# One MoE kernel, four edits: an expert's output rows read, added and written back, a load with another home, a routing step on another engine, and preparation work in other places

## The chip, the core and the metric

The kernel runs on one core of a Trainium2 chip. The metric is the device time of one execution in microseconds (us). The kernel before takes 880.76 us, the median of three runs (879.85 to 880.87). One further execution was profiled; all rows below come from it.

Engines are named as in the profile: PE is TensorE's matmul, PEld its weight load, DVE is VectorE, ACT is ScalarE, POOL is GpSimd, and SP is SyncE, which only issues DMAs here. A "q" behind a name is that engine's sequencer. Each engine works through its own instructions strictly in program order, so an instruction that waits holds everything behind it on its engine.

## The reference, cut to what matters

Three stages follow one another. An attention with 32 memory slots for each head turns q, k, v and phi into 2304 token rows of 512. A gated feed-forward layer (512 to 1536 to 512) follows. Last comes a mixture of eight experts with the two best experts chosen for each token:

```python
logits = x @ w_gate
noisy = logits + log1p(exp(x @ w_noise)) * noise
top2 = argpartition(-noisy, 2, axis=1)[:, :2]     # two experts for each token
top2_w = softmax(noisy[top2])
for e in range(8):
    for k in range(2):
        mask = top2[:, k] == e
        h = maximum(x[mask] @ w1[e], 0)            # 512 -> 1024
        out[mask] += top2_w[mask, k] * (h @ w2[e]) # 1024 -> 512
```

Each token's output row is therefore written by exactly two experts, and the second must add to what the first left.

## The kernel before, in words

**Blocks.** Tokens are worked in NB = 8 blocks of 288. For each block `slot1(i, f)` runs the twelve slices f of the feed-forward layer. Work of neighbouring stages is hung between the matmuls by a hand-written order: `put(i, n, fn, ...)` files a call at place n of block i, and `run(i, n)` issues what is due. Block number 7 is `last`; in it place 2f + 1.99 ends slot f, so 23.9 to 23.95 is the very end of the feed-forward layer.

**Routing** of a block is the list `GATE`: `g_evac`, transposes of the rows (`g_rows`, `g_copy`), logits, a polynomial, the two best experts (`g_top`, `g_pick`), `g_exp`, `g_weight`, `g_spread` (the weights spread over the expert columns of the row tile R, lines 586 to 591), `g_rank` (on PE, line 601: a count of the tokens before each one), `g_place` (lines 604 to 618: the place of each token in its expert's list; line 612 is a product of R on POOL, line 615 overwrites the one-hot tiles that `g_spread` reads), then six `g_scatter` (line 623), indirect DMAs on POOL that write token rows into the expert lists `xs` in DRAM. Each scatter waits for the one before to land. Routing of block k runs inside block k + 1 at the places `AT["gate"][k]`; that of block 7 runs between the units below.

**Units.** Experts 0 and 1 (and the second part of expert 0) are worked in 32 units, `("u", 0)` to `("u", 31)`. A unit is `up2` (line 899: twelve or so products of the expert's first matrix with the transposed rows XT, then the relu on ACT and its low part on DVE, lines 902 and 903) and `down2` of the unit before (line 917). `prep2(n)` (lines 781 to 783) splits the weights for a unit two or more units ahead into a high part on ACT and low parts `ro` and `wl` on DVE. `load_x(e, part)` (lines 847, 849) loads an expert's rows, four DMAs and one for the small columns; `trans_x` and `split_x2` (lines 856, 861, 862) turn and split them. The raw rows of the first parts of experts 0 and 1 share one buffer, tag `xl` of pool `l`, so the second load waits for the transposes of the first. After it on SP's queue stand the weight loads `wb`, before it the stores of row blocks (`store_x`, line 628).

**Pairs.** Experts 2 to 7 take four pairs each, `("s", 0)` to `("s", 23)`; pair p works two slices of expert 2 + p // 4. `pair()` multiplies in a Strassen form (`product`, line 1075) and interleaves the down products (`down_s`, line 1089) of the pair before: `first` and `second` are those. In one pair the order on PE is: two products (A11, S2), `first(0)`, two (A12, S3), `first(1)`, two (S1, A22), `second(0)`, one (S4), `second(1)`. Line 1112 is the ACT copy of the first product, which A12 waits for; line 1115 the DVE sum that S3 waits for; line 1136 the last sum, which the relu at line 1137 waits for. The rows of the expert to come are prepared in these pairs: `load_xs` (lines 972, 975), `trans_xs` (line 984), `sums_xs` on POOL (lines 990 to 994), `high_xs` on ACT (line 1004), `low_xs` on DVE (line 1008); its weights by `sums_ws` (lines 1028 to 1033), `high_ws`, `low_ws`, `high_w2`, `low_w2`.

**Output.** `finish` (line 934 on ACT) scales an output tile and puts it on the list `todo`; `add` (line 941) issues an indirect DMA on POOL that adds the tile to the rows of `out`. Each waits for the one before to land. Expert 7 goes another way: `gather` (line 947) reads the five tiles of old rows into the ring PV, `finish` adds on DVE (line 931), and a plain indirect DMA writes back. The five gathers wait for the last add of expert 6, and the first write waits for all five gathers.

**Homes.** PV is one tile of eight 512-wide rows, tag `X0`, made at the first `rows` call, after the feed-forward layer has read the weights (`places(False)`) that stand under the same tag. Only its rows 0 to 2 are used as a ring at first; rows 3 to 7 take expert 2's raw rows from unit 13 on.

Of the kernel before, what the change touches and what calls it, by code (L numbers as in the profile page):

```python
# [22 lines left out]
DM = 512  # L23
NF1 = 12
E = 8
# [14 lines left out]
    "gate": {  # L40
        0: (3.9, 5.9, 7.9, 7, 9, 9.9, 9.9, 11, 11, 13.9, 15, 15.1, 15.2, 17.9, 25, 27) + NORMAL[16:],
        5: NORMAL[:13] + (15, 17, 19, 21, 21.9, 21.95, 21.96, 23.96, 25, 25.9, 27.9, 29.9, 31.9, 33.9, 35.9),
        6: NORMAL[:13] + (15, 17, 19, 21, 21.9, 21.95, 21.96, 21.97, 23.94),
        7: (1.5, 4, 5, 4.05, 5.05, 6, 3, 6.05, 3.1, 3.5, 3.6, 3.7, 4.1, 5.1, 6.1, 7.1, 7.5, 7.6, 8.1, 8.1, 9, 9.1),
    },
    "s1": {
        1: (21, 21.9, 23.2, 23.5, 23.6, 23.9, 25, 25.9, 27, 27.9, 29, 29.9, 31, 31.9, 33),
# [20 lines left out]
def moe_program(ctx, tc, phi, kv, q, wa, wgn, nz, wb, out):  # L68
# [517 lines left out]
    def g_spread(i):  # L586
        oh1, oh2, sel, w = RT[i]
        s, s2 = small("gs", sh), small("gs2", sh)
        G.tensor_tensor(s, oh1, w[:, 2].to_broadcast(sh), op=OP.mult)
        G.tensor_tensor(s2, oh2, w[:, 3].to_broadcast(sh), op=OP.mult)  # L590
        G.tensor_add(R[i][:, :, DM:DM + E], s, s2)

    PR = {}

# [9 lines left out]
    def g_place(i):  # L604
        oh1, oh2, sel, w = RT.pop(i)
        p = PR.pop(i)
        pos = small("gpos", sh)
        V.tensor_tensor(pos, p[:TT, :NT, :], base[:TT, None, :].to_broadcast(sh), op=OP.add)
        V.tensor_add(base, base, p[:, NT, :])
        ov = R[i][:, :, 528:528 + E]  # L610
        V.tensor_tensor(ov, pos, e_cap[:TT, None, :].to_broadcast(sh), op=OP.is_ge)
        G.tensor_mul(ov, ov, R[i][:, :, DM:DM + E])
        pf = small("gpf", [TT, NT, 2])
        for n, oh in enumerate((oh1, oh2)):
            V.tensor_mul(oh, oh, pos)
# [25 lines left out]
    def put(i, n, fn, *a):  # L641
        fill.setdefault((i, n), []).append((fn, a))
# [196 lines left out]
    def load_x(e, part):  # L839
        (c0, c1), = PARTS[part]  # L840
        pool = pools["l" if part == "a" else "r"]
        XT[e, part] = pool.tile([128, 4, 2, c1 - c0], F32, tag="xt", name="xt", bufs=2)
        if part == "a":
            ML[e] = pools["m"].tile([128, NC, 9], F32, tag="ml", name="ml", bufs=3)
        t = pool.tile([128, (c1 - c0) // 32, 4, 32], F32, tag="xl", name="xl")
        for c in range(4):
            Q.dma_start(t[32 * c:32 * c + 32].rearrange("b j k a -> b j (k a)"),
                        xs[e * T + c0:e * T + c1, 128 * c:128 * c + 128].rearrange("(j b) w -> b j w", b=32))
        Q.dma_start(ML[e][:, c0 // 128:c1 // 128, :],
                    xs[e * T + c0:e * T + c1, DM:DM + 9].rearrange("(c p) w -> p c w", p=128))  # L850
        XL[e, part] = t
# [12 lines left out]
    def index(e, part):  # L864
# [5 lines left out]
            IX[e] = pools["m"].tile([128, NC], I32, tag="ix", name="ix", bufs=3)  # L870
        V.tensor_add(IX[e][:, t], idf, u[:, t])

    def rows(e, part):
        if "all" not in PV:
            PV["all"] = wpool.tile([128, 8, DM], F32, tag="X0", name="pv", bufs=1)
            PV["next"], PV["ring"] = 0, 3
# [43 lines left out]
    def height(e, t):  # L920
        return CAPS - 128 * t if e > 1 and t == NC - 1 else 128
# [3 lines left out]
    def finish(e, tiles):  # L925
        ml = ML[e]
        for t in tiles:
            pv, h = PV[e, t][:height(e, t)], height(e, t)
            w = ml[:h, t, e:e + 1]
            if e == E - 1:  # L930
                V.scalar_tensor_tensor(pv, AC2[e, t][:h], w, pv, op0=OP.mult, op1=OP.add)
                add(e, t)
                continue
            A.activation(pv, AC2[e, t][:h], AF.Copy, scale=w)  # L934
            todo.append((e, t))

    def add(*tile):
        if tile or todo:
# [282 lines left out]
    put(("u", 13), 2.2, load_xs, 2)  # L1221
    for k in range(2):
        for f, h, fn, m in (((17, 1, trans_xs, 0), (18, 1, trans_xs, 1), (18, 2.2, sums_xs, 0), (19, 1, None, 0),
                             (22, 1, None, 1), (22, 1.1, None, 2), (22, 2.3, sums_xs, 1), (23, 1.1, None, 3)),
                            ((23, 2.3, trans_xs, 0), (24, 1, trans_xs, 1), (24, 2.3, sums_xs, 0), (25, 1, None, 0),
                             (26, 1, None, 1), (26, 1.1, None, 2), (26, 2.3, sums_xs, 1), (27, 1.1, None, 3)))[k]:
# [19 lines left out]
    def at(p, h, fn, *a):  # L1246
        put(("s", p), h, fn, *a)

    for p in range(pairs):
# [5 lines left out]
            at(p, 3, load_wb, n + 5)  # L1255
        if p + 1 < pairs:
            at(p, 7, high_w2, p + 1)
        if 0 < p < pairs - 1:
            at(p, 0, sums_ws, p + 1, 0)
            at(p, 0, sums_ws, p + 1, 1)  # L1260
            at(p, 2, sums_ws, p + 1, 2)
            for h, g, k in ((1, 2, "A"), (3, 4, "B"), (3, 5, "C"), (4, 6, "D")):
                at(p, h, high_ws, p + 1, k)
                at(p, g, low_ws, p + 1, k)
        if e + 1 < E:
            if q == 0:
# [158 lines left out]
```

## Time and profile before

| What | Value |
|---|---|
| Median of three runs | 880.76 us (879.85 to 880.87) |
| The profiled execution | 884.36 us |
| Its span, first to last instruction | 882.6 us |
| Mean granted clock of TensorE in the span | 0.983 of full |
| PE busy | 829.9 us (94%) |
| DVE, ACT, POOL busy | 633.2 us, 388.7 us, 242.0 us |

The span is 1.76 us shorter than the profiled execution, and that execution is 3.6 us longer than the median. A busy PE counts the time in which matmuls are in flight. What an idle stretch of an engine costs depends on what waits for it, so the rows are read from PE's own waits backwards.

### The profile page before, as it was taken

Reading aid. Unit: us, or ns where it says so; the run is one execution under the profiler, and the core shown is the slowest. Engines: PE = TensorE matmul, PEld = TensorE weight load, DVE = VectorE, ACT = ScalarE, POOL = GpSimd, SP = SyncE. Lnnn points to the kernel's source line nnn. Section 1 sums busy time; section 2 is a strip of 40 time slices with the busy share of each in tenths; the row PEclk is TensorE's granted clock in tenths of the full one; section 3 lists DMA queues with packets and bytes.
Section 4 is the critical chain, followed back from the end, with each engine's and each line's share of the span. In section 5 each row is a group of like instructions: output and inputs, shape, how many; then the busy total and the mean of one; then the engine's idle time right before and its main releaser. Section 6 shows DMA issues by size and latency. Waiting matters only on the chain.

```text
span 882.6 us, 16296 instructions
## 1 busy us (share of the span) xinstructions
PE 829.9 (94%) x6136; PEld 734.9 (83%) x6136; DVE 633.2 (72%) x1522; ACT 388.7 (44%) x797; POOL 242.0 (27%) x347
## 2 busy tenths in 40 slices
PE   5898999999999999999979999799999999999992
PEld 2676888899989999899869889688888888888881
DVE  4786587676867586857754576688889988888750
ACT  4663555343443343333434545355446554544520
POOL 2000012424342342432133142202415233241241
PEclk9999999999999999999999999899999999999997
DMA  9966628874437453477647953526574744653331
GB/s 327 401 253 220 192 101 302 264 250 135 110 79 219 103 145 84 122 213 192 165 134 208 243 162 80 124 82 135 133 165 97 164 122 113 137 132 105 85 80 60
DMA packets 85079, 142.00 MB, mean 161 GB/s; under 512 B 16432, under 2 KB 41232, under 8 KB 84992
## 3 DMA queue, kind: packets, MB, share of 16 engines
q1 hardware_dynamic: 65712, 100.66, 36.9%
q0 software_dynamic: 19280, 40.22, 19.8%
q8 instruction: 50, 0.82, 0.4%
q14 instruction: 37, 0.30, 0.1%
HBM read 104.07 MB, written 36.77 MB: 160 GB/s over the span
## 4 chain that ended last, share of the span: by engine, by line
PE 79%; DMA 8%; DVE 7%; ACT 2%; issue 2%; SPq 1%; POOL 1%; DVEq 0%; POOLq 0%; ACTq 0%
PE acc L1089 19%; PE ph L1075 15%; PE acc L460 13%; PE pg L427 9%; PE pv L427 7%; PE ph L899 4%; PE acc L917 3%; DMA xl<-xs 2%; PE pp L314 2%; PE acc L456 2%; DMA xs<-R,gidx 2%; PE pkv L285 1%; DMA out<-pv,ix 1%; PE pT L482 1%; PE psc L314 1%
## 5 line engine op out<-in xcount | busy, mean ns | idle before, releaser
L1089 PE MATMUL acc<-ws,hs 128*128 128x512 f32 (+1 forms) x690 | 176.1, 396 | 0.0
L1075 PEld LDWEIGHTS ph<-xh,ws 128*128 128x128 f32 x1008 | 152.4, 190 | 15.3 <-ACT y L1112 6.1
L1075 PE MATMUL ph<-xh,ws 128*128 128x308 f32 x1008 | 159.1, 306 | 5.3 <-ACT y L1112 5.2
L1089 PEld LDWEIGHTS acc<-ws,hs 128*128 128x128 f32 (+1 forms) x690 | 123.4, 185 | 24.6
L941 POOL DMA_INDIRECT out<-pv,ix x40 | 67.5, 1688 | 188.6 <-ACT pv L934 84.5
L460 PE MATMUL acc<-a,ro 128*128 128x288 f32 x576 | 116.3, 294 | 0.0
L427 PE MATMUL pg<-x,pt 128*128 128x288 f32 x576 | 103.3, 314 | 6.4 <-ACT pt L395 4.4
L460 PE MATMUL acc<-a,os 128*128 128x288 f32 x432 | 105.8, 294 | 0.8 <-DVE os L409 0.8
L427 PEld LDWEIGHTS pg<-x,pt 128*128 128x128 f32 x576 | 82.3, 191 | 25.0 <-issue 7.0
L427 PE MATMUL pv<-x,pt 128*128 128x288 f32 x576 | 93.2, 298 | 0.0
L460 PEld LDWEIGHTS acc<-a,ro 128*128 128x128 f32 x576 | 92.1, 188 | 0.0
L440 DVE SCALAR_TENSOR_TENSOR ta<-ta,pg 128x288 f32<-128x288 f32 x84 | 37.9, 451 | 66.2 <-ACT ta L435 63.0
L427 PEld LDWEIGHTS pv<-x,pt 128*128 128x128 f32 x576 | 83.0, 191 | 0.0
L623 POOL DMA_INDIRECT xs<-R,gidx x48 | 48.5, 1010 | 98.9 <-DMA xs<-R,gidx 85.0
L460 PEld LDWEIGHTS acc<-a,os 128*128 128x128 f32 x432 | 74.1, 188 | 1.1 <-DVE os L409 1.1
L435 ACT ACTIVATE ta<-pg 128x288 f32<-128x288 f32 x84 | 34.4, 410 | 87.9 <-PE pg L427 87.8
L419 POOL DMA_DIRECT2D os<-osl x72 | 40.6, 564 | 110.2 <-PE acc L460 66.3
L446 ACT ACTIVATE a<-ta 128x288 fp32r<-128x288 f32 x84 | 37.4, 445 | 70.9 <-DVE ta L441 67.1
L899 PE MATMUL ph<-xt,wm 128*128 128x384 f32 (+1 forms) x256 | 59.3, 320 | 2.8 <-ACT xt L861 2.0
L899 PEld LDWEIGHTS ph<-xt,wm 128*128 128x128 f32 x256 | 46.0, 197 | 6.1 <-ACT xt L861 3.0
L899 PE MATMUL ph<-xt,ro 128*128 128x384 f32 (+1 forms) x128 | 40.9, 320 | 5.4 <-DVE ro L782 5.4
L441 DVE TENSOR_TENSOR ta<-ta,pv 128x288 f32<-128x288 f32 x84 | 38.2, 454 | 8.8
(219 smaller groups left out, 1422.3 us busy)
## 6 DMA issues: line engine op xcount, KB each, us to landing
wb<-wb SPq DMA_DIRECT2D x72, 512.0 KB, 4.8
os<-osl POOLq DMA_DIRECT2D x72, 256.0 KB, 3.2
stg<-wa SPq DMA_DIRECT2D x19, 511.8 KB, 10.0
kv<-kv SPq DMA_DIRECT2D x32, 256.0 KB, 5.0
xl<-xs SPq DMA_DIRECT2D x40, 160.0 KB, 6.6
out<-zt SPq DMA_DIRECT2D x1, 5888.0 KB
xd<-R SPq DMA_DIRECT2D x8, 603.0 KB, 4.3
qt<-q SPq DMA_DIRECT2D x8, 576.0 KB, 7.6
```

The lines of the kernel that those rows point to most:

```text
L419: G.dma_start(r(lo), r(osl[f][:, :]))
L427: P.matmul(p, r(PT[f // 2, g][:, w, f % 2, 128 * a:128 * a + 128]), r(X[i][:, s, g, :]), start=(g == 0 and n == 0), stop=(g == 1 and n == 2))
L435: A.activation(ta, pg, AF.Tanh, scale=0.5)
L440: V.scalar_tensor_tensor(ta, ta, 1.0, pg, op0=OP.add, op1=OP.mult)
L441: V.tensor_mul(ta, ta, pv)
L446: A.activation(r(ah[:, 0, :]), ta, AF.Copy)
L460: P.matmul(ACC[i][c], r(OS[i, f][w][:, o]), r(ah[:, s, :]), start=(f == 0 and n == 0), stop=(f == NF1 - 1 and n == 2))
L623: G.indirect_dma_start(out=xs[:, :], out_offset=bass.IndirectOffsetOnAxis(ap=RT[i][:, t, n:n + 1], axis=0), in_=R[i][:, t, :], in_offset=None)
L899: P.matmul(p, r(w[:, c]), r(x[:, k, b, :]), start=(m == 0), stop=(m == 11))
L941: G.indirect_dma_start(out=out, out_offset=bass.IndirectOffsetOnAxis(ap=IX[e][:h, t:t + 1], axis=0), in_=PV[e, t][:h], in_offset=None, com ...
L1075: P.matmul(out, r(w[i][:, c + 128 * k:c + 128 * k + 128]), r(x[:, m, k, a]), start=(start and n == 0), stop=(n == 5), skip_group_check=not ...
L1089: P.matmul(AC2[e, t][:h], r(a[:, n, o]), r(w[b][:, n]), start=(f == 0 and m == 0), stop=(f == NF2 - 1 and m == 2))
```

## The change

Four edits, and places that go with them.

1. **Expert 6 by gather, add and plain write.** `finish` puts tiles on `todo` for experts 0 to 5 only. Expert 6's five old tiles are gathered in pair 19 (place 5.5) into a new tile `GO` in the `xl` slot of pool `s2`. `add_old` adds a gathered tile to the scaled one on DVE and writes it with a plain indirect DMA, at places 6.5, 7.5, 7.5 of pair 20 and 0.5, 0.5 of pair 21. Expert 7's gather stays in pair 22 (place 0.5).
2. **Expert 1's first load.** It moves from unit 0 (0.1) to the end of the last block (23.9), in front of the stores of place 23.95, and its raw rows go to rows 3 to 5 of PV. PV is therefore made there (`ring`).
3. **Last block's routing.** `g_spread` (three operations) and the product in `g_place` go from POOL to DVE for block 7. The steps of its routing from `g_ratio` on get other places; `g_rank` and `g_place` go behind the weight preparation of unit 4. `g_rank` of block 6 goes from 21.97 to 22.5.
4. **Expert 3's rows.** The two transposes of its first half leave pair 0 for pair 1 (4.1 and 5.1), with the splits behind them in pairs 1 and 2. The weight sums for pair 2 go from pair 1 to pair 0. In units 23 and 24 one `high_xs` and its `low_xs` of expert 2 go one unit later, and a transpose from 2.3 to 2.2.

```diff
         6: NORMAL[:13] + (15, 17, 19, 21, 21.9, 21.95, 21.96, 22.5, 23.94),
-        7: (..., 3.6, 3.7, 4.1, 5.1, 6.1, 7.1, 7.5, 7.6, 8.1, 8.1, 9, 9.1),
+        7: (..., 3.6, 3.7, 4, 4.01, 5.2, 6.1, 7.1, 7.2, 7.6, 7.7, 9.5, 9.6),
...
     def g_spread(i):
-        G.tensor_tensor(s, oh1, w[:, 2].to_broadcast(sh), op=OP.mult)
-        G.tensor_tensor(s2, oh2, w[:, 3].to_broadcast(sh), op=OP.mult)
-        G.tensor_add(R[i][:, :, DM:DM + E], s, s2)
+        eng = V if i == NB - 1 else G
+        eng.tensor_tensor(s, oh1, w[:, 2].to_broadcast(sh), op=OP.mult)
+        eng.tensor_tensor(s2, oh2, w[:, 3].to_broadcast(sh), op=OP.mult)
+        eng.tensor_add(R[i][:, :, DM:DM + E], s, s2)
...
-        G.tensor_mul(ov, ov, R[i][:, :, DM:DM + E])
+        (V if i == NB - 1 else G).tensor_mul(ov, ov, R[i][:, :, DM:DM + E])
...
-        t = pool.tile([128, (c1 - c0) // 32, 4, 32], F32, tag="xl", name="xl")
+        if (e, part) == (1, "a"):
+            ring()
+            t = PV["all"][:, 3:6, :].rearrange(...)
+        else:
+            t = pool.tile([128, (c1 - c0) // 32, 4, 32], F32, tag="xl", name="xl")
...
+    def ring():
+        PV["all"] = wpool.tile([128, 8, DM], F32, tag="X0", name="pv", bufs=1)
+        PV["next"], PV["ring"] = 0, 3
...
-            todo.append((e, t))
+            if e < E - 2:
+                todo.append((e, t))
...
     def gather(e):
+        if e < E - 1:
+            GO["all"] = pools["s2"].tile([128, 2, 10, 4, 32], F32, tag="xl", name="go").rearrange(...)
         for t in range(NC):
             h = height(e, t)
-            G.indirect_dma_start(out=PV[e, t][:h], out_offset=None, in_=out,
+            to = PV[e, t] if e == E - 1 else GO["all"][:, t]
+            G.indirect_dma_start(out=to[:h], out_offset=None, in_=out,
...
+    def add_old(e, t):
+        h = height(e, t)
+        V.tensor_add(PV[e, t][:h], PV[e, t][:h], GO["all"][:h, t])
+        add(e, t)
...
-    put(("u", 0), 0.1, load_x, 1, "a")
+    put(last, 23.9, load_x, 1, "a")
...
-                             (22, 1, None, 1), (22, 1.1, None, 2), (22, 2.3, sums_xs, 1), (23, 1.1, None, 3)),
-                            ((23, 2.3, trans_xs, 0), ...
+                             (22, 1, None, 1), (22, 1.1, None, 2), (22, 2.3, sums_xs, 1), (24, 1.1, None, 3)),
+                            ((23, 2.2, trans_xs, 0), ...
...
-        if 0 < p < pairs - 1:
-            at(p, 0, sums_ws, p + 1, 0)
-            at(p, 0, sums_ws, p + 1, 1)
-            at(p, 2, sums_ws, p + 1, 2)
+        if p == 0:
+            for m in range(3):
+                at(p, (0, 0, 2)[m], sums_ws, 2, m)
+        elif p < pairs - 1:
+            if p > 1:
+                at(p, 0, sums_ws, p + 1, 0)
+                at(p, 0, sums_ws, p + 1, 1)
+                at(p, 2, sums_ws, p + 1, 2)
...
+            if e == 2 and q < 3:
+                places_x = ((), ((4.1, trans_xs, 0, 0), (5.1, trans_xs, 0, 1), (5.2, sums_xs, 0, 0),
+                                 (6.1, high_xs, 0, 0), (7.1, low_xs, 0, 0), (7.1, high_xs, 0, 1),
+                                 (7.1, high_xs, 0, 2)),
+                            ((0.1, low_xs, 0, 1), (0.1, low_xs, 0, 2), (0.2, sums_xs, 0, 1), (2.1, high_xs, 0, 3),
+                             (3.1, low_xs, 0, 3), (4.1, trans_xs, 1, 0), (7, trans_xs, 1, 1)))[q]
...
-        for n in range(5 if p == pairs - 4 else p < pairs - 4):
-            at(p, 6.5 if n < 3 else 7.5, add)
-        at(p, 2.5, add)
+        if p < pairs - 4:
+            at(p, 2.5, add)
+            at(p, 6.5, add)
+        elif p == pairs - 4:
+            for t in range(NC):
+                put(("s", p + (t > 2)), (6.5, 7.5, 7.5, 0.5, 0.5)[t], add_old, e - 1, t)
...
+        if p == pairs - 5:
+            at(p, 5.5, gather, E - 2)
```

## Rows read from the trace of the kernel before

**Rows 1.** PE's waits, whole span: who waited for whom, us total, times, longest.

```profile
PE ph L899 <- DVE ro L782: 5.4, 1, 5.4
...
PE ph L1075 <- ACT y L1112: 5.2, 2, 5.0
...
PE ph L899 <- ACT xt L861: 2.0, 1, 2.0
PE prk L601 <- DVE gsel L571: 1.8, 2, 0.9
...
PE ph L899 <- DVE ta L441: 0.6, 1, 0.6
```

**Rows 2.** Windows: length, busy PE PEld DVE ACT POOL, granted clock, DMA share, GB/s.

```profile
447.80:453.25 5.45, 0.03 (x1) 0.00 (x0) 1.46 (x7) 0.00 (x0) 2.31 (x6) 0.99 0.26 76
453.25:456.60 3.35, 3.35 (x11) 3.35 (x12) 3.17 (x7) 1.99 (x3) 0.95 (x1) 0.51 0.49 154
...
521.35:523.31 1.96, 0.00 (x0) 0.00 (x0) 0.02 (x1) 1.02 (x2) 0.85 (x2) 1.00 0.77 117
524.11:528.46 4.35, 4.35 (x21) 3.93 (x19) 2.70 (x5) 0.39 (x1) 1.98 (x2) 0.61 0.02 4
...
558.00:562.97 4.97, 0.00 (x1) 0.00 (x1) 3.02 (x5) 1.77 (x4) 1.81 (x2) 0.94 0.55 66
562.97:569.20 6.23, 6.16 (x19) 5.12 (x20) 6.20 (x12) 3.80 (x8) 1.18 (x1) 0.50 0.32 112
```

**Rows 3.** Timeline of POOL, 800 us on: start, duration, instruction, [idle before, releaser].

```profile
818.13 2.04 POOL L941 DMA_INDIRECT out<-pv,ix  x1 [13.97 <-ACT pv L934]
...
850.09 1.18 POOL L947 DMA_INDIRECT pv<-out,ix  x1 [4.43 <-DMA out<-pv,ix]
...
859.87 1.03 POOL L941 DMA_INDIRECT out<-pv,ix  x1 [3.47 <-DMA pv<-out,ix]
...
874.64 1.01 POOL L941 DMA_INDIRECT out<-pv,ix  x1 [2.59 <-DMA out<-pv,ix]
```

**Rows 4.** Timeline of DVE, 806 us on: first and last output tile of expert 7.

```profile
853.68 0.75 DVE L931 SCALAR_TENSOR_TENSOR pv<-acc,ml,pv 128x512 f32<-128x512 f32 x1 [1.93 <-DMA pv<-out,ix]
...
866.53 0.75 DVE L931 SCALAR_TENSOR_TENSOR pv<-acc,ml,pv 104x512 f32<-104x512 f32 x1 [3.39 <-PE acc L1089]
```

**Rows 5.** Timelines of DVE and ACT, pairs 0 and 1.

```profile
559.95 0.84 DVE L984 STREAM_TRANSPOSE xr<-xl 128x640 f32<-128x640 f32 x1 [4.48 <-DMA ml<-xs]
...
561.20 0.46 ACT L1137 ACTIVATE hs<-y 128x308 fp32r<-128x308 f32 x1 [6.55 <-DVE y L1136]
```

**Rows 6.** Timeline of DVE, pairs 20 and 21.

```profile
818.03 0.69 DVE L1055 TENSOR_TENSOR ws<-ts,ws 128x512 fp32r<-128x512 f32 x1
...
822.41 0.48 DVE L1115 TENSOR_TENSOR y<-ph,y 128x308 f32<-128x308 f32 x1 [0.88 <-ACT y L1112]
```

**Rows 7.** Line 941 in the whole span: issue to landing.

```profile
DMA to landing us min/median/max: 2.7/5.7/8.4
```

**Rows 8.** Timeline of DVE, units 0 to 8: the place step of the last block.

```profile
451.69 0.19 DVE L615 TENSOR_TENSOR goh<-goh,gpos 96x24 f32<-96x24 f32 x1 [8.12 <-POOL gs L589]
```

**Rows 9.** Timeline of POOL, the same stretch: scatters of blocks 6 and 7.

```profile
431.36 1.00 POOL L623 DMA_INDIRECT xs<-R,gidx  x1 [10.16 <-ACT hh L902]
...
451.42 0.24 POOL L589 TENSOR_TENSOR gs<-goh,gw 96x24 f32<-96x24 f32 x1
...
454.16 0.95 POOL L623 DMA_INDIRECT xs<-R,gidx  x1 [1.71 <-DVE wl L783]
```

**Rows 10.** Timeline of SP, the same stretch: stores of blocks, expert 1's first load.

```profile
411.23 10.35 SPq L628 DMA_DIRECT2D xd<-R  x2
421.74 3.24 SPq L847 DMA_DIRECT2D xl<-xs  x4
```

**Rows 11.** Timelines of POOL and ACT, units 21 to 24.

```profile
518.97 1.55 POOL L941 DMA_INDIRECT out<-pv,ix  x1 [5.59 <-DMA out<-pv,ix]
...
522.24 0.72 ACT L1004 ACTIVATE xh<-sx 128x616 fp32r<-128x616 f32 x1 [2.86 <-POOL sx L994]
```

More of the change, by code (lines that the diff above doesn't have):

```diff
@@ L42 @@
         5: NORMAL[:13] + (15, 17, 19, 21, 21.9, 21.95, 21.96, 23.96, 25, 25.9, 27.9, 29.9, 31.9, 33.9, 35.9),
-        6: NORMAL[:13] + (15, 17, 19, 21, 21.9, 21.95, 21.96, 21.97, 23.94),
-        7: (1.5, 4, 5, 4.05, 5.05, 6, 3, 6.05, 3.1, 3.5, 3.6, 3.7, 4.1, 5.1, 6.1, 7.1, 7.5, 7.6, 8.1, 8.1, 9, 9.1),
+        6: NORMAL[:13] + (15, 17, 19, 21, 21.9, 21.95, 21.96, 22.5, 23.94),
+        7: (1.5, 4, 5, 4.05, 5.05, 6, 3, 6.05, 3.1, 3.5, 3.6, 3.7, 4, 4.01, 5.2, 6.1, 7.1, 7.2, 7.6, 7.7, 9.5, 9.6),
     },
@@ L844, in load_x @@
             ML[e] = pools["m"].tile([128, NC, 9], F32, tag="ml", name="ml", bufs=3)
-        t = pool.tile([128, (c1 - c0) // 32, 4, 32], F32, tag="xl", name="xl")
+        if (e, part) == (1, "a"):
+            ring()
+            t = PV["all"][:, 3:6, :].rearrange("p a w -> p (a w)").rearrange("p (j k a) -> p j k a", k=4, a=32)
+        else:
+            t = pool.tile([128, (c1 - c0) // 32, 4, 32], F32, tag="xl", name="xl")
         for c in range(4):
@@ L871, in index @@
         V.tensor_add(IX[e][:, t], idf, u[:, t])
+    def ring():
+        PV["all"] = wpool.tile([128, 8, DM], F32, tag="X0", name="pv", bufs=1)
+        PV["next"], PV["ring"] = 0, 3
     def rows(e, part):
-        if "all" not in PV:
-            PV["all"] = wpool.tile([128, 8, DM], F32, tag="X0", name="pv", bufs=1)
-            PV["next"], PV["ring"] = 0, 3
         for t in TILES[part]:
@@ L942, in add @@
                                  in_=PV[e, t][:h], in_offset=None, compute_op=OP.bypass if tile else OP.add)
+    GO = {}
     def gather(e):
+        if e < E - 1:
+            GO["all"] = pools["s2"].tile([128, 2, 10, 4, 32], F32, tag="xl", name="go").rearrange(
+                "p i j k a -> p (i j k a)").rearrange("p (t w) -> p t w", t=NC)
         for t in range(NC):
             h = height(e, t)
-            G.indirect_dma_start(out=PV[e, t][:h], out_offset=None, in_=out,
+            to = PV[e, t] if e == E - 1 else GO["all"][:, t]
+            G.indirect_dma_start(out=to[:h], out_offset=None, in_=out,
                                  in_offset=bass.IndirectOffsetOnAxis(ap=IX[e][:h, t:t + 1], axis=0))
+    def add_old(e, t):
+        h = height(e, t)
+        V.tensor_add(PV[e, t][:h], PV[e, t][:h], GO["all"][:h, t])
+        add(e, t)
     A11, A12, A22, S1, S2, S3, S4 = range(7)
@@ L1223, in moe_program @@
         for f, h, fn, m in (((17, 1, trans_xs, 0), (18, 1, trans_xs, 1), (18, 2.2, sums_xs, 0), (19, 1, None, 0),
-                             (22, 1, None, 1), (22, 1.1, None, 2), (22, 2.3, sums_xs, 1), (23, 1.1, None, 3)),
-                            ((23, 2.3, trans_xs, 0), (24, 1, trans_xs, 1), (24, 2.3, sums_xs, 0), (25, 1, None, 0),
+                             (22, 1, None, 1), (22, 1.1, None, 2), (22, 2.3, sums_xs, 1), (24, 1.1, None, 3)),
+                            ((23, 2.2, trans_xs, 0), (24, 1, trans_xs, 1), (24, 2.3, sums_xs, 0), (25, 1, None, 0),
                              (26, 1, None, 1), (26, 1.1, None, 2), (26, 2.3, sums_xs, 1), (27, 1.1, None, 3)))[k]:
@@ L1269, in moe_program @@
                 at(p, 5.5, index, e + 1, "ab")
-            for h, fn, k, m in {0: ((6, trans_xs, 0, 0), (7, trans_xs, 0, 1)),
+            if e == 2 and q < 3:
[4 more added lines that the diff above has]
+                             (3.1, low_xs, 0, 3), (4.1, trans_xs, 1, 0), (7, trans_xs, 1, 1)))[q]
+            else:
+                places_x = {0: ((6, trans_xs, 0, 0), (7, trans_xs, 0, 1)),
                                 1: ((0, sums_xs, 0, 0), (1.1, high_xs, 0, 0), (2.1, low_xs, 0, 0),
@@ L1278, in moe_program @@
                                     (4.1, low_xs, 1, 2), (4.2, sums_xs, 1, 1), (6.1, high_xs, 1, 3),
-                                    (7.1, low_xs, 1, 3))}[q]:
+                                    (7.1, low_xs, 1, 3))}[q]
+            for h, fn, k, m in places_x:
                 at(p, h, fn, e + 1, k, m)
```

## The prediction

> **What bounds the kernel now.** PE is in flight for 94% of the span (the table above), so I read no averages but first PE's waits over the whole span [rows 1]. Behind the feed-forward layer they are few: 5.4 us for a weight part that DVE makes (`ro`), 5.0 us (the longest of two, 5.2 together) for an ACT copy, 2.0 us for a split of rows, two of at most 0.9 us for the routing's rank. Then I read windows at those places [rows 2], since a stall also costs what follows it. [...] The work lost there is 3.35 x 0.49 = 1.6, 6.23 x 0.50 = 3.1 and 4.35 x 0.39 = 1.7. So the three stalls cost 5.4 + 1.6 = 7.0, 5.0 + 3.1 = 8.1 and 2.0 + 1.7 = 3.7 us. Last I read the end on POOL and DVE [rows 3, 4]: the last output tile is ready at 866.53 + 0.75 = 867.28, but its write goes out at 874.64, because the first write waited until 859.87 for expert 7's gathers, the gathers until 850.09 for expert 6's last add, and the five adds began at 818.13. A stall's duration and a queue's order, not busy time, are what this change can move.
>
> **Expert 6 by gather, add and plain write.** Removed: five adding DMAs, whose issues and landings take 850.09 - 818.13 = 32.0 us, 6.4 each [rows 3]. Added: five gathers (the five of expert 7 take 859.87 - 850.09 = 9.8 us up to the first write behind them), five DVE sums of two 128x512 tiles, 0.69 each by the same shape and kind [rows 6], and five plain writes. Those of expert 7 stand 874.64 - 859.87 = 14.8 over four steps, 3.7 us apart [rows 3]. Pairs are (818.13 - 559.95) / 20 = 12.9 us long [rows 3, 5], so the gathers, at 5.5 of pair 19, go out near 805 and land near 815. Expert 5's adds are out by then; their places end in pair 18. The first sum comes where the first add is now, so the writes go out from about 819.5 to 819.5 + 4 x 3.7 = 834.3, and expert 7's gathers start near 838 and end near 848, before the first tile is due. That tile's sum waits 1.93 us for the gather now [rows 4]; without it, it would end near 852.5. Five writes 3.7 apart from 852.8 reach 867.6, and the last tile is ready at 867.3: the last write goes out near 867.7 instead of 874.64. Gain **6.9 us**, none of it on PE. There is slack: plain writes 5 us apart in pairs 20 and 21 would still let the gathers land before the first write is due.
>
> The five sums put 5 x 0.69 = 3.4 us on DVE, whose queue they hold up: behind the first is the last sum of pair 20 (line 1136, then ACT's relu), behind the last two the sum of line 1115 in pair 21, which PE's fourth product waits for. That sum now waits 0.88 us for ACT [rows 6], so part of the two falls into a wait. Bounds: nothing, or the 1.4 us of the two sums; I take nothing, as nine down products on PE lie between. The wait of the gathers for expert 5's adds holds up nothing: POOL has no other work in pair 19 behind them.
>
> [...]
>
> **Expert 1's first load and the last block's routing.** The first stall is a chain: PE waits for `ro`, DVE stands 8.12 us in the place step because its one-hot tile is still to be read by POOL's spread [rows 8], and POOL does that spread only at 451.42, behind six scatters of block 6 that began at 431.36 after 10.16 us of idleness [rows 9]. These wait for expert 1's load, which reads the list that they write; the load starts at 421.74 behind two stores that hold SP for 10.35 us [rows 10]. The row names ACT as releaser of the 431.36 scatter, but ACT's part is long done; the load's landing fits, 9.6 us after its start. The change cuts it twice. On DVE the spread no longer waits for POOL: four more operations of about 0.19 [rows 8], 0.8 us, in a stretch where DVE stood 8.12. And the load moves ahead of the stores, into a home that is free once the last slot's weights are read. SP now has a new wait there, for PE; it falls after 411.23, when SP comes to this place, and before 421.74. I take 413.5, as those products open the last slot, and with the same 9.6 us the load lands near 423, when the scatters' places are known, so they start some 8 us earlier. Nobody waits for the stores behind it on SP; the weight loads behind those come no later. Gain **7.0 us**, and **0.9** for the rank of block 7, which moves behind products. The rank of block 6 gives nothing: PE's next wait there, 0.6 us for the gate's product on DVE [rows 1], grows by as much.
>
> What is late next: weight parts, place step, transposes and splits now run in one piece on DVE, where they ran after the stall. By my count of these operations each `ro` comes about 1 us before PE wants it. Bounds 0 to 1 us for each of four units; I take 0.5 in all. Block 7's scatters, first at 454.16 [rows 9], start some 7.5 us earlier while PE gains 7.9: what hangs on them, the loads of second parts, keeps its margin within 0.5 us.
>
> **Expert 2's split and expert 3's rows.** The second stall: an add at 518.97 held POOL for the one before it, the sums behind it ended late, and ACT stood 2.86 us for them [rows 11] ahead of the split that PE wanted. The split goes first now; ACT meets the sums a unit later (2.8 us), when they are done. One transpose on DVE (line 984) still waits for them, with a unit's relu part queued behind it. Gain 3.7, less 0 to 1; I take **3.4**.
>
> The third: expert 3's first transpose in pair 0 stood 4.48 us on its load, landed only at 559.95, ahead of pair 0's last sum; ACT's relu came 6.55 us late and the copy for pair 1 behind it [rows 5]. DVE came to it at 555.5. Up to place 4.1 of pair 1 stand eight more DVE operations, some 4.7 us (estimate by the 0.48 and 0.69 of rows 6), and the PE work that they wait for, so DVE is there near 561, a microsecond after the landing. Their 2 x 0.84 us, two low parts and the weight sums change pairs: the weight sums (one operation like the 0.69 of rows 6, two of half) fall in pair 0's start, where DVE waits for PE. Nothing is added in sum. Gain **8.1 us**, less 0 to 3 if the landing slips behind 561 or the low parts crowd pair 2; I take 7.6.
>
> **The sum.** 6.9 + 7.0 + 0.9 - 0.5 + 3.4 + 7.6 = 25.3. The profiled execution becomes 884.36 - 25.3 = 859.1 (span 857.3). It lay 3.6 us above the median; scaled, 880.76 x 859.1 / 884.36 = 855.6. I say 855.5.
>
> **Rivals.**
> *Plain writes are as slow as adds* because traffic, not adding, sets the pace. Then expert 6's five take 32.0 us again from 819.5, the gathers 9.8 from 851.5, and the last write leaves at 861.3 + 4 x 3.7 = 876.1, 1.5 later than now instead of 6.9 earlier: 864. Against it: the 2.7 us landings are all plain. [...]
> *The load doesn't come free early* (its home is held longer, or it lands no sooner among other DMAs). DVE's wait is gone, but block 7's scatters keep near 454 while PE is 8 us ahead, and the second load of expert 1 becomes the wait, up to 8 us less a few of slack: about 860 to 862.
> *A new wait in pairs 1 and 2 or in units 5 to 8*: the transposes still wait for their load, or DVE runs without slack. 1 to 5 us with the slower clock after it: 857 to 861.
> *Slower than before*: the gathers of expert 6 land late, and DVE stands in pair 20 with PE's sums behind it. An idle microsecond costs 8.1 / 5.0 = 1.6 at the third stall, so 25.3 us need a wait of 16: landing after 835, though gathers are issued near 805 and take 10. It decides only if expert 5's adds ran 20 us late.
>
> **How the numbers follow.** The sum as worked out 0.62; a new wait 0.16; slow plain writes 0.09; load not early 0.09; slower 0.02; nearly nothing 0.02. If nothing is lost the first gains 26.6 (854.3), and the smaller waits could add 2 to 3 (851.5). Its unknown costs are at most 4 + 1 + 3 + 1.4 = 9.4 us, of which I took 1.3; all of them would give 863.6. The range 851.5 to 863 takes in these, the new wait and part of the two at 860 to 864, and leaves out under 0.2. About 0.2% (1.8 us) is what a measurement of this kernel can tell from no change: faster 0.96, same 0.02, slower 0.02.
>
> **What would show it.** In the changed profile: no DVE wait on POOL's spread and none of PE on `ro`; block 6's scatters from about 423; no ACT wait for the sums before the split; no DVE wait on expert 3's load in pair 0, and no window at half clock in units or pairs; plain writes of expert 6 near 3.7 us apart, and the last write within 1 us of the last tile. Wrong would be: a new PE wait over 2 us between units 5 and 16 or in pairs 1 to 3, or a last write that still trails its tile by 5 us.

## The result and the profile after

The changed kernel takes 859.56 us (median of four runs, 858.91 to 860.38) where the kernel before takes 880.31 (879.20 to 880.87): a ratio of 0.977, 95% interval 0.975 to 0.978, or 20.75 us less. The forecast of 855.5 was 4.1 us too low; its range of 851.5 to 863 holds the time. The profiled execution after took 859.25 us, its span 857.5.

PE's waits of the kernel after, whole span (who waited for whom, us in total, times, longest):

```profile
PE ph L905 <- DVE ta L441: 1.5, 1, 1.5
...
PE ph L905 <- DVE xt L867: 1.0, 1, 1.0
...
PE ph L1093 <- DVE y L1133: 0.6, 1, 0.6
...
PE ph L1093 <- DVE v L1139: 0.5, 1, 0.5
```

Of [rows 1] the waits for `ro` (5.4), for the copy `y` (5.0), for ACT's part of a split (2.0) and for the rank (1.8) are gone. The first wait above, for the gate's product, is the 0.6 us of [rows 1] grown by block 6's rank, as forecast. The other three, 1.0, 0.6 and 0.5 us on DVE, are new, and the sum did not hold them.

The chain of the first stall in the timelines of the kernel after (start, duration, instruction, idle time before and what ended it). SP:

```profile
412.41 1.86 SPq L852 DMA_DIRECT2D pv<-xs  x4
```

POOL, with the first scatter of block 6 and of block 7:

```profile
421.54 0.99 POOL L624 DMA_INDIRECT xs<-R,gidx  x1 [1.33 <-DVE hl L909]
...
447.04 1.21 POOL L624 DMA_INDIRECT xs<-R,gidx  x1 [5.97 <-DVE xu L861]
```

DVE, the place step:

```profile
443.63 0.17 DVE L616 TENSOR_TENSOR goh<-goh,gpos 96x24 f32<-96x24 f32 x1
```

Against [rows 8 to 10]: expert 1's load starts at 412.41 instead of 421.74, block 6's scatters at 421.54 instead of 431.36, block 7's at 447.04 instead of 454.16, and DVE's place step waits for nobody. The forecast had 413.5, about 423, and 7.5 us earlier.

The end, from POOL's timeline:

```profile
800.66 1.02 POOL L948 DMA_INDIRECT out<-pv,ix  x1 [7.87 <-DVE pv L965]
804.24 1.26 POOL L948 DMA_INDIRECT out<-pv,ix  x1 [2.56 <-DVE pv L965]
...
817.87 1.05 POOL L948 DMA_INDIRECT out<-pv,ix  x1 [2.59 <-DVE ws L1084]
821.36 1.38 POOL L960 DMA_INDIRECT pv<-out,ix  x1 [2.45 <-DMA out<-pv,ix]
...
834.70 1.03 POOL L948 DMA_INDIRECT out<-pv,ix  x1 [6.48 <-DVE pv L937]
...
848.83 1.01 POOL L948 DMA_INDIRECT out<-pv,ix  x1 [2.60 <-DVE pv L937]
```

Expert 6's plain writes stand (817.87 - 800.66) / 4 = 4.3 us apart, where the adds stood 6.4 apart [rows 3]. So expert 7's gathers are done before its first tile, and its last write now waits for DVE's last tile instead of trailing it by 7.4 us.

PE runs the same 6136 matmuls in every kernel here, so the time between the same two of them can be set side by side. The table is worked out from the traces. The marks are the matmuls that began at 408.0, 475.1, 519.2, 535.0, 550.1 and 600.1 us in the profile of before; "tail" runs from the end of the last matmul to the end of the span. The stretches not shown take 281.5 us together in every kernel.

| Kernel | to 408 | 408 to 475 | 475 to 519 | 519 to 535 | 550 to 600 | tail | span |
|---|---|---|---|---|---|---|---|
| before, first profile | 408.0 | 67.1 | 44.1 | 15.8 | 50.0 | 16.1 | 882.6 |
| before, profiled again | 407.8 | 67.2 | 44.3 | 13.6 | 49.3 | 16.2 | 879.9 |
| expert 6 alone | 408.0 | 66.5 | 43.4 | 13.5 | 49.8 | 9.6 | 872.3 |
| load and routing alone | 406.6 | 58.3 | 44.1 | 13.6 | 49.9 | 15.8 | 869.7 |
| expert 2's and 3's rows alone | 407.3 | 68.0 | 43.4 | 12.1 | 43.2 | 16.0 | 871.4 |
| load alone | 409.0 | 59.4 | 43.4 | 13.9 | 49.8 | 15.9 | 872.6 |
| routing alone | 408.7 | 59.5 | 53.4 | 16.4 | 50.0 | 14.4 | 883.8 |
| after | 407.0 | 58.7 | 44.1 | 13.0 | 43.2 | 9.9 | 857.5 |
| after, profiled again | 408.8 | 58.3 | 45.2 | 13.0 | 43.3 | 10.0 | 860.1 |
| after, two moves | 406.5 | 58.3 | 43.9 | 11.9 | 42.4 | 9.8 | 854.3 |
| after, three moves | 408.3 | 58.4 | 45.6 | 11.9 | 41.7 | 9.9 | 857.3 |

The stretch up to 408, which no edit touches, spreads over 2.5 us from one execution to the next, and 475 to 519 over 2.2 (routing alone set aside). So single spans say little below 2 to 3 us. Of the four columns with the edits three are steadier: kernels that are alike in that part agree within 1.5 us there (the tail of the routing alone, 14.4, set aside). The fourth, 519 to 535, is not: without its edit it takes 13.5 to 16.4.

### The profile page after: what moved, and what is told of

Same layout as the page of the kernel before. It is cut to its first block, busy times and chain, and to the rows that moved or that the text cites. A ratio compares the mean times of both kernels' runs of the same rounds, so it can differ in the third digit from the quotient of the medians.

```text
span 857.5 us, 16316 instructions
## 1 busy us (share of the span) xinstructions
PE 822.5 (96%) x6136; PEld 729.4 (85%) x6136; DVE 639.1 (75%) x1531; ACT 389.0 (45%) x797; POOL 245.9 (29%) x348
## 4 chain that ended last, share of the span: by engine, by line
PE 78%; DVE 10%; DMA 5%; ACT 3%; issue 2%; SPq 0%; POOL 0%; DVEq 0%; POOLq 0%; ACTq 0%
PE acc L1107 17%; PE ph L1093 16%; PE acc L460 13%; PE pg L427 9%; PE pv L427 7%; PE ph L905 4%; PE acc L923 3%; PE pp L314 2%; DMA out<-pv,ix 2%; PE acc L456 2%; PE pkv L285 2%; PE pT L482 1%; DMA xl<-xs 1%; PE psc L314 1%; DVE xt L867 1%
## 5 line engine op out<-in xcount | busy, mean ns | idle before, releaser
L948 POOL DMA_INDIRECT out<-pv,ix x40 | 64.5, 1614 | 175.7 <-ACT pv L940 70.2
L905 PE MATMUL ph<-xt,wm 128*128 128x384 f32 (+1 forms) x256 | 57.3, 312 | 2.6 <-DVE ta L441 1.5
L905 PEld LDWEIGHTS ph<-xt,wm 128*128 128x128 f32 x256 | 44.1, 189 | 5.5 <-ACT xt L866 1.7
L447 DVE TENSOR_TENSOR a<-ta,a 128x288 fp32r<-128x288 f32 x84 | 37.4, 445 | 6.6 <-ACT a L446 6.3
```

Source lines behind the costliest of these rows:

```text
L447: V.tensor_sub(r(ah[:, 1, :]), ta, ah[:, 0, :])
L905: P.matmul(p, r(w[:, c]), r(x[:, k, b, :]), start=(m == 0), stop=(m == 11))
```

## The experiments

**The kernel before, once more.** Where did the 3.6 us lie by which the first profile exceeded the median?

> The kernel before, unchanged, profiled a second time. Its profiled execution took 884.36 us, 3.6 above the median of the timed runs, and the forecast scaled this excess away evenly. Theory A (the excess sits in the stalls that the change removes): the new execution is near 880, the waits and slow-clock stretches at 447.8, 521.4 and 558.0 cost together some 3 to 4 us less than the 18.8 us that were counted, and all other stretches agree within 0.5 us. Rival B (the excess is spread): the three stalls cost 18.8 us within 1 us again, and the rest of the span is shorter by about 0.4%.

It took 881.71 us, its span 879.9. PE's waits in it:

```profile
PE ph L899 <- DVE ro L782: 5.5, 1, 5.5
...
PE ph L1075 <- ACT y L1112: 5.2, 2, 4.9
...
PE ph L899 <- ACT xt L861: 1.3, 1, 1.3
```

Windows behind the three stalls, the second first (length, busy PE, PEld, DVE, ACT, POOL, granted clock, DMA share, GB/s):

```profile
523.50:528.00 4.50, 4.50 (x29) 3.98 (x28) 3.70 (x7) 1.78 (x4) 2.00 (x2) 1.00 0.02 4
...
453.09:456.50 3.41, 3.41 (x11) 3.41 (x12) 3.23 (x7) 1.99 (x3) 0.94 (x1) 0.50 0.49 162
...
560.80:567.00 6.20, 6.13 (x22) 5.24 (x23) 6.17 (x12) 3.80 (x8) 1.18 (x1) 0.60 0.33 114
```

POOL's timeline, the add ahead of the second stall:

```profile
518.22 1.55 POOL L941 DMA_INDIRECT out<-pv,ix  x1 [4.77 <-ACT xh L1004]
```

The first stall costs what it did, the third 0.7 us less (50.0 to 49.3 in the table), and the clock behind them is 0.50 and 0.60, where it was 0.51 and 0.50 [rows 2]. The second did not: the add that holds POOL went out at 518.22 instead of 518.97 [rows 11], PE's wait was 1.30 instead of 1.96, and behind it the clock stayed at 1.00 where it had been 0.61 for 4.35 us [rows 2]. In the table the stretch 519 to 535 falls from 15.8 to 13.6, which is 2.2 of the 2.7 us between the two spans. So theory A has the place right, but the three stretches together fall by 2.8 us instead of 3 to 4, and most of that lies at one stall. Three single parts below agree, with 13.5, 13.6 and 13.9 in that stretch where the edit there is absent; the routing alone, with a wait of 2.56 there, has 16.4.

**Each part alone.** The edits are the parts 1, 2 with 3, and 4 of the diff, each put into the kernel before without the others.

> Of the four edits expert 6's gather, add and plain write alone. Theory A (the tail is a queue of DMAs of fixed lengths): 6.9 us faster than before, that is a ratio near 0.992; plain writes of expert 6 stand 3.5 to 4.5 us apart and the last write leaves within 1 us of the last output tile. Rival B (the missing 4 us of the whole gain are missing here, since the five sums hold DVE up or the tail was shorter in the timed runs): 3 us, ratio 0.9965.

> Expert 1's early load from a free home and the last block's routing on VectorE, with the routing's places, alone. By the forecast 7.0 + 0.9 - 0.5 = 7.4 us faster, ratio 0.9916. Theory A (the excess of the profiled execution lay in its stalls, this one among them): 5 to 7.4 us. Rival B (the clock window behind this stall is not there in timed runs, and new small waits take the rest): under 4 us, ratio above 0.9955.

> Expert 2's split in units 23 and 24 and expert 3's rows and weight sums in other pairs, alone. By the forecast 3.4 + 7.6 = 11.0 us faster, ratio 0.9875. Theory A (the stall at the start of the pairs hangs on a load whose landing differs between executions; the profiled one was a bad one): 6 to 8 us, ratio 0.991 to 0.993. Rival B (the stalls are the same in all executions): 11.0 us.

| Part | Ratio, 95% interval | Gain of 881.34, us | Forecast |
|---|---|---|---|
| expert 6 | 0.993 (0.991 to 0.995) | 6.3 (4.7 to 7.8) | 6.9 |
| load and routing | 0.991 (0.989 to 0.994) | 7.8 (5.7 to 9.9) | 7.4 |
| expert 2's and 3's rows | 0.991 (0.990 to 0.993) | 7.7 (6.3 to 9.0) | 11.0 |

The parts add up: 6.3 + 7.8 + 7.7 = 21.8, near the 20.75 of the whole. Two came as forecast. The third is short by 3.3 us, theory A of its expectation in size. Its reason is only half right: it named the stall at the start of the pairs as the one that differs between executions, and the profiles put most of that on the second stall.

**Is the chain cut twice?** The forecast said that expert 1's load and the last block's routing both cut it, and gave them one sum.

```diff
 load alone:    hunks of load_x, ring and put(last, 23.9, load_x, 1, "a"); spread and product stay on G
 routing alone: hunks of g_spread, g_place and the places of blocks 6 and 7; load_x stays at ("u", 0), 0.1
```

> Expert 1's first load alone goes to the free home ahead of the stores; the last block's routing stays on GpSimd, at its old places. Theory A (one chain that is cut twice, so either cut frees it): block 6's scatters start near 421.5 instead of 431.4, the spread follows them near 442 instead of 451.4, about when VectorE comes to it, PE's wait for ro falls from 5.4 to under 1 us, and the kernel is 6 to 7 us faster. Rival B (the two edits add up): the spread is still late for VectorE, the wait is 2 to 4 us, the gain 2 to 4 us.

> The last block's spread and product on VectorE and the routing's places alone; expert 1's first load stays behind the stores, in its old home. Theory A (either cut frees the chain): VectorE no longer waits for GpSimd, PE's wait for ro is gone, block 7's scatters stay near 454 as GpSimd is held by block 6's, and the loads of second parts have slack enough: 6 to 8 us faster. Rival B (late scatters give it back): a new PE wait of 3 us or more stands between units 8 and 16, and the gain is under 4 us.

The load alone gives a ratio of 0.992 (0.989 to 0.994), 7.1 us; the routing alone 0.998 (0.996 to 1.000), 1.7 us with an interval that reaches zero. With the load alone, POOL's timeline:

```profile
423.05 0.99 POOL L623 DMA_INDIRECT xs<-R,gidx  x1 [1.33 <-DMA xd<-R]
...
442.26 0.94 POOL L623 DMA_INDIRECT xs<-R,gidx  x1 [4.04 <-DMA xs<-R,gidx]
443.24 0.23 POOL L589 TENSOR_TENSOR gs<-goh,gw 96x24 f32<-96x24 f32 x1
```

and DVE's:

```profile
443.98 0.17 DVE L615 TENSOR_TENSOR goh<-goh,gpos 96x24 f32<-96x24 f32 x1
```

POOL's spread, at 443.24 to 443.96, is done just as DVE comes to its place step; PE has no wait on `ro` at all. With the routing alone, PE's waits:

```profile
PE acc L918 <- DVE hl L904: 7.1, 2, 6.4
```

DVE's timeline at that wait:

```profile
489.03 0.45 DVE L857 STREAM_TRANSPOSE xu<-xl 128x256 f32<-128x256 f32 x1 [11.44 <-DMA xl<-xs]
```

POOL's, the first scatter of block 7:

```profile
456.80 0.92 POOL L624 DMA_INDIRECT xs<-R,gidx  x1 [2.79 <-DVE ro L783]
```

and windows of PE's wait and of what follows it (columns as above):

```profile
483.56:489.90 6.34, 0.00 (x0) 0.00 (x0) 0.87 (x2) 0.39 (x2) 1.59 (x1) 0.77 1.08 248
489.90:500.00 10.10, 10.03 (x45) 8.80 (x46) 8.11 (x19) 5.47 (x11) 1.74 (x1) 0.81 0.95 207
```

The stall at 447.8 is gone here too (59.5 us in 408 to 475), but block 7's scatters begin at 456.80, and the load of expert 1's second part, which reads the lists that they write, lands 11.44 us after DVE is ready for it. PE stands 6.41 us and runs at 0.81 behind that: the stretch 475 to 519 grows by 9.3. This is the forecast's rival "the load doesn't come free early", shown with its mechanism. The profiled execution (885.61) was the longest of ten (875.38 to 885.61), so the new wait is probably shorter in most; only this one was profiled. So the two edits are not two cuts of equal worth: the load cuts the chain alone, and the routing alone only moves the wait. With the load early, the routing still takes away the rank's two waits (0.8 and 0.9 us), which the load alone keeps; one of them comes back as a longer wait for the gate's product (0.2 to 1.1), and 408 to 475 takes 58.3 us with both against 59.4. Nor do block 6's scatters wait for the early load any more. Whatever releaser the rows name, the first of them goes out 0.88 us behind the end of DVE's cast of its places, at 420.66 in the changed kernel and at 422.17 with the load alone.

**Adding or traffic?** The rival on plain writes is told apart by changing nothing but the kind of expert 6's writes.

```diff
-                                 in_=PV[e, t][:h], in_offset=None, compute_op=OP.bypass if tile else OP.add)
+                                 in_=PV[e, t][:h], in_offset=None, compute_op=OP.bypass if tile or e == E - 2 else OP.add)
```

> The kernel before, with the five writes of expert 6 plain instead of adding, nothing gathered or added in their place (expert 6's sum with the older rows is left out, so its time is that of a kernel that does less). Theory A (an adding write is slow by its kind): steps of 3.5 to 4.5 us instead of 6.4, expert 7's gathers from about 838 instead of 850 on that profile's scale, and a last write within 1 us of the last tile. Rival B (the traffic around sets the pace): steps of 6 us or more and the same tail as before.

POOL's timeline (one execution, 873.98 us):

```profile
814.34 1.47 POOL L941 DMA_INDIRECT out<-pv,ix  x1 [13.97 <-ACT pv L934]
...
831.58 1.00 POOL L941 DMA_INDIRECT out<-pv,ix  x1 [2.62 <-ACT ws L1051]
835.10 1.23 POOL L947 DMA_INDIRECT pv<-out,ix  x1 [2.52 <-DMA out<-pv,ix]
...
864.13 1.01 POOL L941 DMA_INDIRECT out<-pv,ix  x1 [2.71 <-DVE pv L931]
```

Same places, same rows, same neighbours: (831.58 - 814.34) / 4 = 4.3 us a step instead of 6.4, and the last write leaves 1.4 us after PE's last product instead of 8.2. The profile tells the landing of some issues only; of the third and the fifth write it does in both kernels. Line 941 in 833 to 846 us of the kernel before, as adds, and in 823 to 832 us here, as plain writes:

```profile
DMA to landing us min/median/max: 4.6/5.2/5.8
```
```profile
DMA to landing us min/median/max: 3.2/3.2/3.3
```

So the kind makes the difference: 3.2 and 3.3 us where the adds took 4.6 and 5.8. Plain writes differ among themselves too: in the changed kernel those of expert 7, at the end, land after 2.7 to 2.8 us, with a DMA share of 0.26 meanwhile, and one of expert 6 (804.24) after 5.0, with a share of 0.53. Whether the traffic makes that difference was not tried.

**What the small waits are.** After the change, PE waits 1.0 us at 512.1 for the low part of a split. DVE's timeline there, at the start of the pairs, and in pairs 1 and 2:

```profile
511.54 1.51 DVE L867 TENSOR_TENSOR xt<-xu,xt 128x256 fp32r<-128x256 f32 x1 [0.48 <-ACT xt L866]
...
537.61 0.69 DVE L1046 TENSOR_TENSOR ts<-wb 128x512 f32<-128x512 f32 x1 [2.99 <-PE acc L923]
...
546.68 1.21 DVE L1084 TENSOR_TENSOR ws<-wb,ws 128x1024 fp32r<-128x1024 f32 x1
...
559.05 0.47 DVE L1133 TENSOR_TENSOR y<-ph,y 128x308 f32<-128x308 f32 x1
559.44 1.71 DVE L1084 TENSOR_TENSOR ws<-wb,ws 128x1024 fp32r<-128x1024 f32 x1
561.06 1.07 DVE L1051 TENSOR_TENSOR ts<-wb,ts 128x256 f32<-128x256 f32 x1
```

POOL's timeline of the same kernel:

```profile
510.56 1.42 POOL L1011 TENSOR_TENSOR sx<-xr 128x308 f32<-128x308 f32 x1
511.37 1.39 POOL L1012 TENSOR_TENSOR sx<-xr,sx 128x308 f32<-128x308 f32 x1
...
559.21 0.85 POOL L1011 TENSOR_TENSOR sx<-xr 128x308 f32<-128x308 f32 x1 [3.29 <-DVE xh L1026]
...
560.02 1.84 POOL L1012 TENSOR_TENSOR sx<-xr,sx 128x308 f32<-128x308 f32 x1
```

The splits before this one took 0.42. This one ends at 513.05, 0.29 after POOL's second sum (512.76). Expert 2's and 3's rows alone have the same meeting, but a shorter one. DVE and POOL there:

```profile
520.10 0.80 DVE L862 TENSOR_TENSOR xt<-xu,xt 128x256 fp32r<-128x256 f32 x1 [0.48 <-ACT xt L861]
```
```profile
519.77 0.84 POOL L994 TENSOR_TENSOR sx<-xr,sx 128x308 f32<-128x308 f32 x1
```

The split ends at 520.90, again 0.29 after the sum (520.61), and PE's wait for it is at most 0.2, so that this stretch took 12.1 us there and 13.0 in the whole change. Ahead of the sums POOL issues an add. In that run it was done at 518.12, 0.7 us before the DVE operation that the sums wait for; in the changed kernel it was done at 511.08, 0.7 behind that operation, so that the sums met the split in full.

In pair 2 the two engines take turns: DVE's 1.21 us operation (546.68, nothing on POOL) takes 1.71 as POOL's first sum is running; POOL's second sum, 0.85 like the first, takes 1.84 until 561.86, behind that operation's end at 561.15; and DVE's next ends at 562.13, 0.27 after it. The sum `y`, with one operand from PSUM, took its usual 0.47 although POOL's first sum began within it, and that sum its 0.85. What the two engines share there no run shows; the rows show the lengths alone.

```diff
# two moves
-                at(p, (0, 0, 2)[m], sums_ws, 2, m)
+                at(p, 2, sums_ws, 2, m)
...
-    (22, 2.3, sums_xs, 1)   # on G
+    (23, 2.15, sums_xs, 1)  # on V, behind the last split
# third move
-                             (3.1, low_xs, 0, 3), (4.1, trans_xs, 1, 0), (7, trans_xs, 1, 1)))[q]
+                             (4.05, low_xs, 0, 3), (4.1, trans_xs, 1, 0), (7, trans_xs, 1, 1)))[q]
```

> The changed kernel with two more moves. First, the first two weight sums for pair 2 go behind the sum that PE's fourth product of pair 0 waits for: the wait of 0.55 us at 538.7 goes. Second, the two sums of expert 2's rows that GpSimd does beside the last split go to VectorE, behind that split. Theory A (GpSimd and VectorE keep each other off a shared resource, which made the split 1.51 us instead of 0.42): the split takes 0.42 to 0.5 us again and PE's wait of 1.0 us at 512.1 goes; the VectorE sums cost 2 x 0.5 us where nobody waits; in all 1.5 us faster than the changed kernel, about 858. Rival B (the split was long for another reason, such as the transpose or a DMA beside it): the split stays over 1 us, and only 0.5 us are gained.

> The changed kernel, unchanged, beside the kernels with moves, so that all stand on the same chip. By its first runs 0.977 of the kernel before. Theory A (its first profile was typical): the split beside GpSimd's sums is 1.2 to 1.6 us long again, PE waits 0.9 to 1.1 us there and 0.55 us in pair 0; its granted clock stays near 1.00 after both. Rival B (chance of one execution): one of these waits is missing.

> The changed kernel with three moves: the two of the run before (weight sums behind the sum of pair 0's fourth product; two sums of expert 2's rows on VectorE), and the low part of expert 3's rows in pair 2 (0.79 us) behind the sum v that PE's sixth product waits for. Theory A (VectorE is the late one there, as GpSimd's sums stretch its 0.42 and 1.21 us operations to 1.07 and 1.71): PE's wait of 0.47 us at 560 goes, the stretch of pairs 2 and 3 that took 25.8 us takes 25.1 to 25.3, and the kernel is 0.5 us faster than with two moves, 2 to 2.5 us faster than the changed one. Rival B (another operand is late too): the wait moves to the next product and nothing is gained.

DVE's timeline with two moves:

```profile
510.40 0.42 DVE L867 TENSOR_TENSOR xt<-xu,xt 128x256 fp32r<-128x256 f32 x1 [0.48 <-ACT xt L866]
510.74 0.47 DVE L1011 TENSOR_TENSOR sx<-xr 128x308 f32<-128x308 f32 x1
...
534.28 0.48 DVE L1133 TENSOR_TENSOR y<-ph,y 128x308 f32<-128x308 f32 x1 [1.90 <-PE ph L1093]
```

The same of the changed kernel, profiled again:

```profile
514.36 1.11 DVE L867 TENSOR_TENSOR xt<-xu,xt 128x256 fp32r<-128x256 f32 x1 [0.48 <-ACT xt L866]
```

The split is back at 0.42, `y` waits for PE instead of PE for it, and both waits are gone: 11.9 instead of 13.0 us in 519 to 535, and 42.4 instead of 43.2 in 550 to 600, the stretch that holds pair 0's wait; 1.9 together, where 1.5 was expected. The second profile of the changed kernel has them all again; its split took 1.11, below the expected 1.2, and PE's wait there 0.76 instead of 0.9 to 1.1. With the third move, DVE in pair 2:

```profile
561.63 1.07 DVE L1051 TENSOR_TENSOR ts<-wb,ts 128x256 f32<-128x256 f32 x1
...
563.23 0.47 DVE L1139 TENSOR_TENSOR v<-ph,y 128x308 f32<-128x308 f32 x1
```

and POOL:

```profile
560.59 1.83 POOL L1012 TENSOR_TENSOR sx<-xr,sx 128x308 f32<-128x308 f32 x1
```

The engines still hold each other up there (1.07 and 1.83), and ahead of `v`; but the low part of 0.79 us no longer stands there too, PE's wait for `v` is gone, and the stretch 550 to 600 falls by another 0.7 to 41.7. On one chip, with 881.38 for the kernel before, the changed kernel took 861.36 (0.977, 0.975 to 0.978) and that with three moves 858.69 (0.974, 0.972 to 0.975): 2.7 us less than the changed kernel, where 2 to 2.5 was expected. It beats both kernels. Two moves gave 0.974 (0.972 to 0.976) on another chip, so the times do not show what the third move alone is worth; the stretch does.

## Why the prediction was right, and where its 4 us went

The direction and the range held, and each of the four parts gained by the mechanism that the forecast gave it; the time was 4.1 us too low. The terms beside the profiles, each worked out from the table of stretches:

| Term | Forecast | First profile of before | Profiled again |
|---|---|---|---|
| tail | 6.9 | 16.1 - 9.9 = 6.2 | 16.2 - 9.9 = 6.2 |
| first stall, rank, less new waits | 7.0 + 0.9 - 0.5 = 7.4 | 67.1 - 58.7 = 8.4 | 67.2 - 58.7 = 8.5 |
| second stall | 3.4 | 15.8 - 13.0 = 2.8 | 13.6 - 13.0 = 0.6 |
| third stall | 7.6 | 50.0 - 43.2 = 6.8 | 49.3 - 43.2 = 6.1 |
| to 408, 475 to 519 | 0 | 1.0 | 1.0 |
| sum | 25.3 | 25.1 | 22.4 |

*The step that failed is the scaling.* "It lay 3.6 us above the median; scaled, 880.76 x 859.1 / 884.36 = 855.6" took the excess of one execution off evenly. From that profile to the one after, the sum is right: 25.3 forecast, 25.1 measured, and 859.1 forecast for the profiled execution against 859.25. That it fits so closely is luck: tail, second and third stall fall short by 0.6 to 0.8 us each, the first stall gives 1.0 more, and stretches that no edit touches happened to be 1.0 shorter. But of the 2.7 us between the two profiles of before, 2.2 lie in the stretch of the second stall. The change removes that stall, and the forecast counted its full price as gain and then took the same excess off once more. Left unscaled, it would have been 859.1; the median is 859.56.

*Second stall: the term that was mis-sized.* "Gain 3.7, less 0 to 1; I take 3.4" priced it by an execution with a wait of 1.96 us and a clock of 0.61 behind it. The second profile, and those of expert 6 alone, of load and routing and of the load alone, have waits of 1.1 to 1.5 there and 13.5 to 13.9 us in the stretch instead of 15.8; behind the wait the clock was 1.00 in both windows read there (the second profile, the load alone). So the 1.7 us of the clock were not there to be won. Of the rest, about 1 us went to the split that POOL's sums stretch: with those moved the stretch takes 11.9, and the gain on the second profile is 1.7 instead of 0.6.

*Third stall: mechanism right, price short by two waits.* DVE no longer waits for expert 3's load in pair 0. But that the weight sums "fall in pair 0's start, where DVE waits for PE", failed: the first of them waits itself for PE's last product of the units (2.99 us, until 537.61), so they run behind that wait and ahead of `y`, and PE waits 0.55. And "the low parts crowd pair 2", which stood as a bound, came true, with POOL's sums as its second cause. With the three moves the stretch is 41.7, and the gain on the second profile 49.3 - 41.7 = 7.6.

*First stall: right.* It gave about 1 us more than the sum, as the 0.5 allowed for new waits on `ro` did not come; the rest is of the size by which this stretch differs between kernels with both edits (58.3 to 58.7). What the forecast did not see is that the load alone carries the 7.0, with the routing left the 0.9 of the rank, and that the routing without the load makes the wait of its own rival.

*Tail: right.* The last write left 8.15 us after PE's last end before (874.64 - 866.49) and leaves 1.30 after it now (848.83 - 847.53): 6.85 of the 6.9 forecast. What follows the last write took 7.9 to 8.6 us in all profiles but that of the routing alone (6.4), and 8.6 in this one, so the column shows 6.2. The five sums on DVE cost PE nothing, as forecast: from 600 us to its last product PE takes 266.4 us in every kernel here. The steps were 4.3 instead of the 3.7 assumed; the slack that the forecast named, up to 5 us, covered that.

*Rivals.* The likeliest case (0.62) and "a new wait in pairs 1 and 2 or in units 5 to 8" (0.16) share the result: three waits of 0.5 to 1.0 us came, at the last split, in pair 0 and in pair 2, and 859.6 lies in that rival's 857 to 861. Only the wait in pair 2 stands where that rival had looked for one. That plain writes are as slow as adds is ruled out by the run that changes only their kind (steps of 4.3 us instead of 6.4). The 2.7 us landings that the forecast held against it are the least of [rows 7]: two writes of expert 7 landed after 2.8 and 2.7 (859.87 and 867.59), the ten adds whose landing the profile tells after 4.6 to 8.4. That the load doesn't come early is shown to cost what was feared by the routing alone.

What stays open: why the add ahead of the second stall went out 0.75 us later in the first profile (it waits there for the add before it to land), and what makes the stretch up to 408 differ by up to 2.5 us between executions. Neither was tried.

## What to carry to other kernels

A stall that hangs on when a DMA lands had no fixed price here (the second one's stretch took 15.8 and 13.6 us in two profiles of the same kernel): profile the kernel twice before costing it, and take the excess of a long execution off the stretch where it lies instead of scaling it. When a chain is cut at two places, ask of each cut alone what is late next, since one may do all the work and the other only move the wait. Two operations on VectorE and GpSimd that nobody has put in each other's way in the code can still be so, as the split here, 1.51 us instead of 0.42 beside POOL's sums: look at both timelines for a row two or three times its usual length before taking a place on either engine as free.

## What was not expected of the hardware

GpSimd's sums of 0.85 us cost VectorE more than they would have cost on VectorE itself: 0.5 + 0.65 = 1.15 us of stretching in pair 2 (1.21 to 1.71 and 0.42 to 1.07) against 2 x 0.47 for the same kind of sum moved there. And the clock behind a stall did not go by the place: at one and the same product, after waits of 1.30 us (the second profile of before) and 1.52 us (the load alone) the granted clock was 1.00 in the windows behind, of 4.50 and 4.40 us; after 1.96 (the first profile of before) and 2.56 (the routing alone) it was 0.61 and 0.62 in windows of 4.35 and 4.30. Between the two profiles of before the wait differs by 0.7 us (1.30 and 1.96) and the stretch 519 to 535 by 2.2 (13.6 and 15.8). What sets the clock there no run shows. Two windows behind that product, the load alone (after 1.52) and the routing alone (after 2.56):

```profile
516.10:520.50 4.40, 4.40 (x28) 3.88 (x27) 3.62 (x7) 1.68 (x4) 2.00 (x2) 1.00 0.02 4
```
```profile
526.90:531.20 4.30, 4.30 (x20) 3.90 (x20) 2.84 (x5) 0.39 (x1) 1.81 (x2) 0.62 0.02 4
```

In nearly the same time, 4.4 and 4.3 us, PE did 28 matmuls in the first and 20 in the second.
